# Gated linear attention beside a bilinear GLU: a new order for one unit's ScalarE and VectorE work

## The chip, the cores and the metric

The kernel runs on one core of a Trainium2 chip. The metric is the device time of one execution in microseconds (us), as the median of several runs. The engines are TensorE (PE in the profile; PEld is its loading of stationary operands), VectorE (DVE), ScalarE (ACT), GpSimd (POOL) and SyncE (SP). SP and POOL do almost nothing here but issue DMAs.

## The reference

The input `x` has 2048 rows of 512 numbers. Two branches read it, and a gate mixes them:

```
g = sigmoid((x * gate_w).sum(-1))
a = linear attention(x; wqkv, wo)        # 32 heads of 16; phi(t) = where(t > 0, t+1, exp(t)) + 1e-6
b = ((x @ w_gate) * (x @ w_up)) @ w_down # 512 -> 1792 -> 512
out = g * a + (1 - g) * b
```

All of it is float32. The linear attention needs `kv = phi(k)^T v` and `z = sum phi(k)` over all rows before any query can be finished; a query's result is `phi(q) kv / (phi(q) z)`.

## The kernel before, in words

**Precision.** A float32 operand is split into a high part, which TensorE's fast format `fp32r` can hold, and a low remainder. A split is one ACT instruction (`hi = src`) and one DVE instruction (`lo = src - hi`), and a product is three matmuls (`mm3`: high by high, low by high, high by low). So every operand that TensorE reads costs ACT and DVE something first.

**Phase 1** (to 93.85 us of the profiled span) goes over the 16 row tiles and builds `pk = phi(x wk)` and the four banks `gt = pk^T x`. It opens with `WARM` dummy matmuls on zeros (line 184) while the first weights arrive.

**Phase 2** is a list of 32 **units** (`order`, lines 124 to 130). The 2048 rows are taken as two pairs of chunks of 2 x 512 rows; for each pair there are 14 units of kind "f" (one 128-wide slice of `w_gate` and `w_up`) with two units of kind "q" (query weights) among them, at places 6 and 11. A unit (line 387) multiplies a 2 x 2 block matrix of weights with a 2 x 2 block matrix of `x` in the seven products of a Strassen-like scheme; the sums of blocks that it needs are formed by DMAs that add in flight. The names of the products and the PSUM banks they go to, in PE's order, are

| product | bank | what it needs first | what reads the bank |
|---|---|---|---|
| 2 | Y | | ACT `m2` (named `m` in the profile) |
| 3 | X | | DVE `R = X - m2` |
| 4 | Y | `m2` has read Y | ACT `cross[:, 0]` |
| 1 | R | `R` written | DVE `t = R + cross[:, 0]` |
| 5 | X | `R` has read X | DVE `S = t - X`, ACT `cross[:, 1]` |
| 6 | R | `t` has read R | DVE `cross[:, 1] = R * cross[:, 1]`, then `hh[:, 1]` on ACT, `hl[:, 1]` on DVE |
| 7 | S | `S` written | DVE `cross[:, 0] = S * cross[:, 0]`, then `hh[:, 0]` on ACT, `hl[:, 0]` on DVE |

`h` (`hh`, `hl`) is the split hidden state of the unit's 128 columns, chunk 0 and chunk 1. Between the products stand **down jobs** (`down`, line 372; matmuls named `pdn`): two units' `h` times their `w_down` rows for one tile of 128 rows, six matmuls into one bank, added to an accumulator in SBUF by one DVE instruction (`acc`). The eight jobs of two units take the four tiles of chunk 1 first. `shares` says how many jobs follow products 3, 4, 5 and the `S` step of each unit.

**Order.** Every engine executes its instructions in the order in which the program lists them (`pin`). Work that belongs to no product is put at named places of a unit with `later(n, place, fn)` and executed by `do(n, place)`; along a unit the places are e (after `R`), m and c (after product 4), d (before product 1), t (after `t`), s (before the last down jobs), r (between products 6 and 7) and end. The steps that the change touches are

- the weights of later units: `w_load` (SP loads `wr`, three of seven blocks), `w_add` (two ACT instructions make copies and a negative in `wr`, then a POOL DMA adds 640 KB onto it), `w_high` and `w_low` (split into `wch` on ACT and `wcl` on DVE, in three parts; part 2 holds the blocks of products 1, 6 and 7);
- `down_weights` (line 711): the split of the unit's `w_down` rows, `dh` on ACT and `dl` on DVE, at place c, from a single buffer `wdr`, whose next load is issued behind the split;
- the attention of a q unit n (line 567): the query features `phq`, their products with z summed through DRAM (`zq`, `terms`, `zt`), the reciprocal (`recip`, which also writes `den` to DRAM), four broadcast loads `rb` of it (`norm`), and four pairs `norm_high` / `norm_low` that scale and split the features to an `h` of their own;
- the `x` blocks of the second pair: sums formed early by `cb_load`, `x_add` and `cb_split` and parked in DRAM, either split already (`xpark`, two tensors) or not (`xsum`), and loaded during unit 15 (`reload`); those from `xsum` are split during unit 16.

Of the kernel before, what the change touches and what calls it, by code (L numbers as in the profile page):

```python
# [7 lines left out]
F32 = mybir.dt.float32  # L8
F32R = mybir.dt.float32r
AF = mybir.ActivationFunctionType  # L10
ALU = mybir.AluOpType
# [3 lines left out]
P = 128  # L15
S = 2048
D = 512
# [8 lines left out]
NPAIR = NC // 2  # L26
TPP = 2 * CH // P
EPS = 1e-6
WARM = 7
LEAD = 4  # L30
HB = 8
NH = 5
# [11 lines left out]
def gated_mix(ctx: ExitStack, tc, xt, xp, x, wqkv, wq, wq_add, wo, wgu, wgu_add, wdn, gate_w, out):  # L44
# [12 lines left out]
    def act(dst, src, func=AF.Copy, **kw):  # L57
        pin(nc.scalar.activation(dst, src, func, **kw))  # L58

    def tt(dst, a, b, op):  # L60
        pin(nc.vector.tensor_tensor(dst, a, b, op=op))  # L61
# [54 lines left out]
    nc.gpsimd.affine_select(out=m3, in_=m3, compare_op=ALU.is_ge, fill=0.0, base=DH - 1,  # L116
                            pattern=[[DH, P // DH], [0, DH]], channel_multiplier=-1)

    xpark = {i: [dram.tile([P, 2, CH], F32, name=f"xpark{i}{v}") for v in "hl"] for i in (2, 3)}
    xsum = {i: dram.tile([P, 2, CH], F32, name=f"xsum{i}") for i in (4, 1, 5, 6, 7)}  # L120
    wpark = [[dram.tile([P, D], F32, name=f"wpark{b}{v}") for v in "hl"] for b in range(KT)]


# [18 lines left out]
    def w_add(n):  # L142

        if n < len(order):
            _, kind, m = order[n]
            act(raws[n][:, 3:5], raws[n][:, 0:1].to_broadcast([P, 2, 2 * P]))
            act(raws[n][:, 5:7], raws[n][:, 0:2], scale=-1.0)
            dma_add(raws[n][:, 2:7], (wgu_add if kind == "f" else wq_add)[m])
# [3 lines left out]
    def w_high(n):  # L152
        if n < len(order):
            wcs[n] = [const.tile([P, 7, 2 * P], F32R, tag=f"wc{v}", name=f"wc{v}", bufs=2) for v in "hl"]
            for a, b in PARTS:
                act(wcs[n][0][:, a:b], raws[n][:, a:b])

    def w_low(n, part):
        if n < len(order):
            a, b = PARTS[part]  # L160
            tt(wcs[n][1][:, a:b], raws[n][:, a:b], wcs[n][0][:, a:b].bitcast(F32), ALU.subtract)
# [203 lines left out]
    def later(n, place, fn):  # L365
        at.setdefault((n, place), []).append(fn)

    def do(n, place):
        for fn in at.pop((n, place), []):
            fn()  # L370
# [16 lines left out]
    def unit(n, quad):  # L387

        wh, wl = wcs.pop(n)
        bank = {t: psum.tile([P, CH], F32, tag=t, name=f"b{t}") for t in "YXRS"}  # L390

        def reload(i):
            if n + 1 == units and i in xpark:
                for src, part in zip(xpark[i], xc[i]):
                    dma(part.bitcast(F32), src)
            elif n + 1 == units:
                hi, lo = xc[i]
                dma(lo.bitcast(F32), xsum[i])

                def split_there():  # L400
                    act(hi, lo.bitcast(F32))
                    tt(lo, lo.bitcast(F32), hi.bitcast(F32), ALU.subtract)

                later(units, {4: "e", 1: "m", 5: "c", 6: "t", 7: "s"}[i], split_there)

        def product(i, to, start=False):
            for k in range(2):
                ks = slice(k * P, (k + 1) * P)
                mm3(bank[to], (wh[:, SLOT[i], ks], wl[:, SLOT[i], ks]), [v[:, k] for v in xc[i]],
                    start and k == 0, k == 1, not start)  # L410
            reload(i)

        m2 = p2.tile([P, CH], F32, tag="t", name="m2")
        cross = p2.tile([P, 2, CH], F32, tag="cross", name="cross", bufs=2)
        product(2, "Y", True)
        act(m2, bank["Y"])
        product(3, "X", True)

        tt(bank["R"], bank["X"], m2, ALU.subtract)
        do(n, "e")  # L420
        many = share(n)
        down(many[0])
        product(4, "Y")
        act(cross[:, 0], bank["Y"])
        do(n, "m")
        do(n, "c")
        down(many[1])
        do(n, "d")
        w_add(n + 2)
        product(1, "R")  # L430
        t = p2.tile([P, CH], F32, tag="t", name="t")
        tt(t, bank["R"], cross[:, 0], ALU.add)
        if n:
            w_high(n + 1)
        do(n, "t")
        product(5, "X")
        tt(bank["S"], t, bank["X"], ALU.subtract)
        act(cross[:, 1], bank["X"])
        if n:
            w_low(n + 1, 0)  # L440
        down(many[2])
        if quad:
            quad(1, 0, cross[:, 0])
        if n:
            w_low(n + 1, 1)
        do(n, "s")
        down(many[3])
        w_low(n + 1, 2)
        if quad:
            quad(0, 1, cross[:, 1])  # L450
        product(6, "R")
        if quad:
            quad(1, 1, bank["R"])
        else:
            hh, hl = hidden()
            tt(cross[:, 1], bank["R"], cross[:, 1], ALU.mult)
            act(hh[:, 1], cross[:, 1])
        do(n, "r")
        product(7, "S")
        if quad:  # L460
            quad(0, 0, bank["S"])
        else:
            tt(cross[:, 0], bank["S"], cross[:, 0], ALU.mult)
            act(hh[:, 0], cross[:, 0])

            for c in 1, 0:
                def low(c=c):
                    tt(hl[:, c], cross[:, c], hh[:, c].bitcast(F32), ALU.subtract)

                if n + 1 == len(order):  # L470
                    later(n, f"low{c}", low)
                else:
                    low()
            return hh, hl

    def hidden():
# [8 lines left out]
    def wp_load():  # L485
        att["wv"] = [p2.tile([P, D], F32, tag="acc", name="wv", bufs=8) for _ in range(KT)]
        att["wo"] = [p2.tile([P, D], F32, tag="ph", name="wo_sb", bufs=4) for _ in range(KT)]
        for k in range(KT):
            dma(att["wv"][k], wqkv[k * P:(k + 1) * P, 2 * D:3 * D])
        for k in range(KT):  # L490
            dma(att["wo"][k], wo[k * P:(k + 1) * P, :])
# [76 lines left out]
    def attention(pair, j, n):  # L568
# [41 lines left out]
        def norm(i):  # L610
            r, c = parts[i]
            if r not in group:
                group[r] = hidden()
            rb = p2.tile([P, CH], F32, tag="z", name="rb", bufs=4)
            one = there[HB * i:HB * (i + 1)].rearrange("h c t -> h (c t)")
            dma(rb, one[:, None, :].to_broadcast([HB, DH, CH]))
            den[i] = rb
# [26 lines left out]
        for e, place in zip((1, 2, 3), ("s", "s", "end")):  # L644
            later(n + 2, place, lambda e=e: z_add(e))
        later(n + 2, "end", z_end)
        later(n + 3, "e", recip)
        for i in range(4):
            later(n + 3, "m", lambda i=i: norm(i))
        for i, places in enumerate((((n + 3, "r"), (n + 4, "e")), ((n + 4, "m"), (n + 4, "c")),  # L650
                                    ((n + 4, "d"), (n + 4, "t")), ((n + 4, "s"), (n + 4, "r")))):
            for fn, (m, place) in zip((norm_high, norm_low), places):
                later(m, place, lambda i=i, fn=fn: fn(i))
        later(*((n + 5, "e") if turns else (n + 3, "c")), weights)
# [10 lines left out]
    def cb_split(i, k):  # L665
        lo = cb.pop((i, k))
        if i in xsum:
            dma(xsum[i][:, k], lo)
            return
        hi = p2.tile([P, CH], F32R, tag="cb", name="cbh", bufs=3)  # L670
        act(hi, lo)
        tt(lo, lo, hi.bitcast(F32), ALU.subtract)
        dma(xpark[i][0][:, k], hi.bitcast(F32))
        dma(xpark[i][1][:, k], lo)
# [13 lines left out]
    for n, (i, k) in enumerate((i, k) for i in (2, 3, 4, 1, 6, 7) for k in range(2)):  # L688
        later(n, "s", lambda i=i, k=k: cb_load(i, k))
        later(n + 1, "c", lambda i=i, k=k: x_add(cb[i, k], 1, i, k))  # L690
        later(n + 2, "c", lambda i=i, k=k: cb_split(i, k))
    later(1, "r", lambda: dma(xsum[5], xp[1, SUMS[5][1]]))
    wdr = {}

    def d_load(n):
        if n < len(order) and order[n][1] == "q":
            n += 1
        if n < len(order):
            wdr[n] = p2.tile([P, D], F32, tag="wdr", name="wdr")
            dma(wdr[n], wdn[order[n][2]])  # L700

    d_load(0)
    wp_load()
    half = None
    for n, (pair, kind, m) in enumerate(order):
        entry = {}
        if n == 6:

            banks[0] = "att"

        def down_weights(n=n, entry=entry):
            entry["d"] = down_tiles()
            split(*entry["d"], wdr.pop(n))
            d_load(n + 1)

        if kind == "f":
            at.setdefault((n, "c"), []).insert(0, down_weights)
        hid = unit(n, attention(pair, m, n) if kind == "q" else None)
        w_load(n + 3)
        if kind == "f":  # L720
            if half is None:
                half = (hid, entry["d"])
            else:
                jobs += down_jobs(pair, (half, (hid, entry["d"])), ocol)
                half = None
        do(n, "end")
# [56 lines left out]
```

## Time and profile before

| what | value |
|---|---|
| median of 3 runs | 609.63 us (607.29 to 611.16) |
| the profiled execution | 611.52 us, of which the span from first to last instruction is 609.7 us |
| PE busy | 601.4 us, 99% of the span, 2657 matmuls |
| DVE busy | 443.2 us, 73% |
| ACT busy | 311.3 us, 51% |
| granted TensorE clock | 1.000 over the span |
| phase 2, first to last matmul | 93.85 to 606.2 us |

In a group's row the tile that is written stands left of the arrow, what is read right of it; "idle before" is the time for which the engine did nothing ahead of these instructions, with the instruction that ended it. In a timeline a row gives start, duration, engine, line and tiles, and in brackets the idle time ahead of it. Nearly all instructions go through helpers, so a line number tells little (L52 is every matmul, L58 every ACT copy, L61 every DVE subtraction or product) and the tile names have to be read.

### The profile page before, as it was taken

How to read it: one execution, taken by the hardware profiler on the slowest of the kernel's cores; microseconds unless marked ns; L12 is line 12 of the kernel's file. 1: busy time of each engine (PE TensorE's matmuls, PEld its weight loads, DVE VectorE, ACT ScalarE, POOL GpSimd, SP SyncE). 2: the span in 40 equal slices, each digit the busy share in tenths (PEclk: the TensorE clock that was granted, in tenths of full speed). 3: DMA queues.
4: the chain of work that ended last, by engine and by line, in shares of the span. 5: the costliest groups of instructions: out<-in, count | busy, mean ns of one | idle time of the engine just before them, and what ended most of it. 6: DMA issues, size and time to landing. Idle time of an engine off the chain costs nothing.

```text
span 609.7 us, 7505 instructions
## 1 busy us (share of the span) xinstructions
PE 601.4 (99%) x2657; PEld 494.7 (81%) x2657; DVE 443.2 (73%) x690; ACT 311.3 (51%) x533; POOL 46.4 (8%) x62
## 2 busy tenths in 40 slices
PE   9999999999999999899999999999999999999997
PEld 6888888888888888788887788888888887888886
DVE  6877896666776787767887876556677887668874
ACT  3855765476549542564444634664474455643310
POOL 0011100001111110200000012010000000000000
PEclk9999999999999999999999999999999999999999
DMA  9477956667777868857469725334476564552403
GB/s 300 164 186 134 285 147 145 184 173 205 209 186 175 234 130 237 200 131 198 103 148 307 231 95 156 88 90 87 85 188 163 117 166 103 136 138 57 140 0 139
DMA packets 48406, 96.97 MB, mean 159 GB/s; under 512 B 4448, under 2 KB 15456, under 8 KB 48352
## 3 DMA queue, kind: packets, MB, share of 16 engines
q1 hardware_dynamic: 40672, 67.65, 34.1%
q0 software_dynamic: 7408, 28.32, 26.1%
q10 hardware_dynamic: 288, 0.52, 0.3%
q8 instruction: 21, 0.34, 0.2%
q14 instruction: 17, 0.14, 0.1%
HBM read 81.53 MB, written 15.47 MB: 159 GB/s over the span
## 4 chain that ended last, share of the span: by engine, by line
PE 88%; DMA 4%; DVE 4%; ACT 1%; issue 1%
PE pdn L52 28%; PE bR L52 13%; PE bY L52 13%; PE bX L52 13%; PE pk L52 7%; PE gt L52 7%; PE bS L52 6%; DMA wdr<-in_wdn 4%; DVE acc L64 1%; DVE wcl L61 1%; DVE cross L61 1%; PE pkv L52 1%; DMA wraw<-in_wqkv 1%; DVE hl L61 1%; PE pw L52 0%
## 5 line engine op out<-in xcount | busy, mean ns | idle before, releaser
L52 PE MATMUL pdn<-dh,hl 128*128 128x512 f32 x290 | 112.5, 388 | 0.4 <-DVE hl L61 0.4
L52 PE MATMUL pdn<-dh,hh 128*128 128x512 f32 x290 | 112.5, 388 | 0.2 <-ACT hh L58 0.2
L52 PE MATMUL pdn<-dl,hh 128*128 128x512 f32 x290 | 112.4, 388 | 0.0
L58 ACT ACTIVATE hh<-cross 128x512 fp32r<-128x512 f32 x56 | 35.1, 633 | 98.1 <-DVE cross L61 98.1
L64 DVE SCALAR_TENSOR_TENSOR acc<-pdn,ocol,acc 128x512 f32<-128x512 f32 (+1 forms) x97 | 71.0, 738 | 13.2 <-PE pdn L52 11.6
L61 DVE TENSOR_TENSOR wcl<-wr,wch 128x512 fp32r<-128x512 f32 (+1 forms) x96 | 72.9, 773 | 1.8 <-ACT wch L58 1.8
L52 PEld LDWEIGHTS pdn<-dh,hl 128*128 128x128 f32 x290 | 54.4, 188 | 11.9 <-DVE hl L61 0.8
L52 PEld LDWEIGHTS pdn<-dh,hh 128*128 128x128 f32 x290 | 54.5, 188 | 11.8 <-ACT hh L58 0.6
L52 PEld LDWEIGHTS pdn<-dl,hh 128*128 128x128 f32 x290 | 54.5, 188 | 11.2
L58 ACT ACTIVATE wch<-wr 128x512 fp32r<-128x512 f32 (+1 forms) x96 | 60.0, 691 | 0.0
L58 ACT ACTIVATE cross<-bY 128x512 f32<-128x512 f32 x32 | 19.1, 598 | 68.0 <-PE bY L52 68.0
L61 DVE TENSOR_TENSOR dl<-wdr,dh 128x512 fp32r<-128x512 f32 x28 | 19.4, 692 | 44.2 <-ACT dh L58 44.2
L52 PE MATMUL bX<-xbh,wch 128*128 128x512 f32 x128 | 49.8, 389 | 0.0
L52 PE MATMUL bX<-xbh,wcl 128*128 128x512 f32 x128 | 49.8, 389 | 0.0
L52 PE MATMUL bX<-xbl,wch 128*128 128x512 f32 x128 | 49.8, 389 | 0.0
L85 POOL DMA_DIRECT2D wr<-in_wgu_add x28 | 24.3, 866 | 303.4 <-ACT wr L58 186.7
L61 DVE TENSOR_TENSOR hl<-cross,hh 128x512 fp32r<-128x512 f32 x56 | 37.9, 688 | 2.7
L58 ACT ACTIVATE wr<-wr 128x512 f32<-128x512 f32 x64 | 36.6, 622 | 4.4 <-DMA wr<-in_wgu 4.4
L61 DVE TENSOR_TENSOR bR<-bX,m 128x512 f32<-128x512 f32 x32 | 22.3, 697 | 15.2 <-PE bX L52 15.2
L61 DVE TENSOR_TENSOR bS<-t,bX 128x512 f32<-128x512 f32 x32 | 22.2, 695 | 15.1 <-PE bX L52 15.0
L58 ACT ACTIVATE cross<-bX 128x512 f32<-128x512 f32 x32 | 19.0, 593 | 25.1 <-DVE bS L61 25.0
L61 DVE TENSOR_TENSOR t<-bR,cross 128x512 f32<-128x512 f32 x32 | 22.0, 688 | 13.5 <-PE bR L52 13.5
(160 smaller groups left out, 1262.8 us busy)
## 6 DMA issues: line engine op xcount, KB each, us to landing
wr<-in_wgu_add POOLq DMA_DIRECT2D x28, 640.0 KB, 7.5
wr<-in_wgu SPq DMA_DIRECT2D x28, 384.0 KB, 5.7
wdr<-in_wdn SPq DMA_DIRECT2D x28, 256.0 KB, 4.9
xraw<-in_x SPq DMA_DIRECT2D x16, 256.0 KB, 4.8
terms<-zq SPq DMA_DIRECT2D x16, 256.0 KB, 2.3
zt<-terms SPq DMA_DIRECT2D x16, 256.0 KB, 8.2
rb<-den SPq DMA_DIRECT2D x16, 256.0 KB
xtraw<-in_xt SPq DMA_DIRECT2D x12, 256.0 KB, 4.1
```

What stands on the lines that cost most here:

```text
L52: tc.keep_in_program_order(nc.tensor.matmul(*args, **kw))
L58: pin(nc.scalar.activation(dst, src, func, **kw))
L61: pin(nc.vector.tensor_tensor(dst, a, b, op=op))
L64: pin(nc.vector.scalar_tensor_tensor(dst, a, scalar, b, op0=op0, op1=op1))
L85: tc.keep_in_program_order(nc.gpsimd.dma_start(dst, src, accum_op=ALU.add))
```

## The change

No matmul of the computation is added or removed. Within a unit the ACT and DVE work stands in another order:

- `hh[:, 0]` and `hl[:, 0]` of a unit move into the next unit: `hh[:, 0]` behind that unit's `m2`, `hl[:, 0]` behind its `R`. The last unit keeps the old order.
- `down_weights` moves from place c to place e, ahead of whatever else stands there; its load buffer `wdr` becomes two, and each load is issued two f units ahead.
- `w_high` moves ahead of `w_add` and of product 1; `w_low` of part 0 moves from behind product 5 to behind `t`.
- The attention's `recip` moves from place e of unit n + 3 to the end of n + 2, the `rb` loads from m to e, and each `norm_high` / `norm_low` one place or so earlier.
- The `x` block 4 of the second pair is split before it is parked and loaded as two tensors; its split in unit 16 goes. The splits of parked blocks (`cb_split`) move from c to e.
- There are 8 dummy matmuls at the start where there were 7.

```diff
-WARM = 7
+WARM = 8
...
-    xpark = {i: [dram.tile([P, 2, CH], F32, name=f"xpark{i}{v}") for v in "hl"] for i in (2, 3)}
-    xsum = {i: dram.tile([P, 2, CH], F32, name=f"xsum{i}") for i in (4, 1, 5, 6, 7)}
+    xpark = {i: [dram.tile([P, 2, CH], F32, name=f"xpark{i}{v}") for v in "hl"] for i in (2, 3, 4)}
+    xsum = {i: dram.tile([P, 2, CH], F32, name=f"xsum{i}") for i in (1, 5, 6, 7)}
...
-                later(units, {4: "e", 1: "m", 5: "c", 6: "t", 7: "s"}[i], split_there)
+                later(units, {1: "m", 5: "c", 6: "t", 7: "s"}[i], split_there)
...
         product(2, "Y", True)
         act(m2, bank["Y"])
+        do(n, "high")
         product(3, "X", True)
 
         tt(bank["R"], bank["X"], m2, ALU.subtract)
+        do(n, "low")
         do(n, "e")
...
         do(n, "d")
+        if n:
+            w_high(n + 1)
         w_add(n + 2)
         product(1, "R")
         t = p2.tile([P, CH], F32, tag="t", name="t")
         tt(t, bank["R"], cross[:, 0], ALU.add)
         if n:
-            w_high(n + 1)
+            w_low(n + 1, 0)
         do(n, "t")
         product(5, "X")
         tt(bank["S"], t, bank["X"], ALU.subtract)
         act(cross[:, 1], bank["X"])
-        if n:
-            w_low(n + 1, 0)
         down(many[2])
...
             tt(cross[:, 0], bank["S"], cross[:, 0], ALU.mult)
-            act(hh[:, 0], cross[:, 0])
-
-            for c in 1, 0:
-                def low(c=c):
-                    tt(hl[:, c], cross[:, c], hh[:, c].bitcast(F32), ALU.subtract)
-
-                if n + 1 == len(order):
-                    later(n, f"low{c}", low)
-                else:
-                    low()
+
+            def high(c):
+                act(hh[:, c], cross[:, c])
+
+            def low(c):
+                tt(hl[:, c], cross[:, c], hh[:, c].bitcast(F32), ALU.subtract)
+
+            if n + 1 < len(order):
+
+                low(1)
+                later(n + 1, "high", lambda: high(0))
+                later(n + 1, "low", lambda: low(0))
+            else:
+
+                high(0)
+                for c in 1, 0:
+                    later(n, f"low{c}", lambda c=c: low(c))
             return hh, hl
...
-        later(n + 3, "e", recip)
+        later(n + 2, "end", recip)
         for i in range(4):
-            later(n + 3, "m", lambda i=i: norm(i))
-        for i, places in enumerate((((n + 3, "r"), (n + 4, "e")), ((n + 4, "m"), (n + 4, "c")),
-                                    ((n + 4, "d"), (n + 4, "t")), ((n + 4, "s"), (n + 4, "r")))):
+            later(n + 3, "e", lambda i=i: norm(i))
+        for i, places in enumerate((((n + 3, "s"), (n + 3, "r")), ((n + 3, "end"), (n + 4, "e")),
+                                    ((n + 4, "c"), (n + 4, "d")), ((n + 4, "t"), (n + 4, "s")))):
...
-        later(n + 2, "c", lambda i=i, k=k: cb_split(i, k))
+        later(n + 2, "e", lambda i=i, k=k: cb_split(i, k))
...
-    def d_load(n):
-        if n < len(order) and order[n][1] == "q":
-            n += 1
-        if n < len(order):
-            wdr[n] = p2.tile([P, D], F32, tag="wdr", name="wdr")
+    ffn = [n for n, u in enumerate(order) if u[1] == "f"]
+
+    def d_load(i):
+        if i < len(ffn):
+            n = ffn[i]
+            wdr[n] = p2.tile([P, D], F32, tag="wdr", name="wdr", bufs=2)
             dma(wdr[n], wdn[order[n][2]])
 
     d_load(0)
     wp_load()
+    d_load(1)
...
-            d_load(n + 1)
+            d_load(ffn.index(n) + 2)
 
         if kind == "f":
-            at.setdefault((n, "c"), []).insert(0, down_weights)
+            at.setdefault((n, "e"), []).insert(0, down_weights)
```

## The prediction

> **What bounds the kernel now.** I read the busy shares first, then PE's list of waits, then the timelines around each wait.
>
> ```profile
> PE 601.4 (99%) x2657; PEld 494.7 (81%) x2657; DVE 443.2 (73%) x690; ACT 311.3 (51%) x533; POOL 46.4 (8%) x62
> ```
> ```profile
> PE bY L52 <- ACT m L58: 2.1, 2, 1.8
> ...
> PE bY L52 <- DVE xc4l L61: 0.6, 1, 0.6
> PE pdn L52 <- DVE hl L61: 0.4, 1, 0.4
> ```
>
> PE is busy 99% of the span, and the chain of waits shows six matmuls every 1.36 us (0.227 each) from 7.33 us on. The change leaves every real matmul, so only time in which PE does not keep this pace can be won. Start to start, all distances over 0.227 add up to 8.3 us: 3.1 before 7.33 us (slow clock, first weights), 0.5 in six small hitches, and 4.7 in three places of phase 2. Behind PE's last matmul lie 3.5 us of accumulation and output, unchanged. No order of ACT and DVE can win more than 4.7 + 0.5 in phase 2.
>
> ```profile
> 252.72 0.39 PE L52 MATMUL pdn<-dh,hl 128*128 128x512 f32 x1
> 254.87 0.50 PE L52 MATMUL bY<-xc4h,wch 128*128 128x512 f32 x1 [1.77 <-ACT m L58]
> 255.21 0.39 PE L52 MATMUL bY<-xc4l,wch 128*128 128x512 f32 x1
> ...
> 334.93 0.50 PE L52 MATMUL pdn<-dh,hh 128*128 128x512 f32 x1 [0.20 <-ACT hh L58]
> ...
> 336.06 0.50 PE L52 MATMUL pdn<-dh,hl 128*128 128x512 f32 x1 [0.40 <-DVE hl L61]
> ...
> 338.82 0.50 PE L52 MATMUL bY<-xc4l,wch 128*128 128x512 f32 x1 [0.65 <-DVE xc4l L61]
> ...
> 507.94 0.50 PE L52 MATMUL bY<-xc4h,wch 128*128 128x512 f32 x1 [0.31 <-ACT m L58]
> ```
>
> Each stall costs more than its bracket, since the pipeline refills. At 254.87: 255.21 - 252.72 is 2.49 for two steps of 0.227, so 2.03 lost. The other places, counted so: 1.15 (334.34 to 336.40), 0.92 (338.82) and 0.59 (507.94). Together 4.7. They are the starts of units 11, 16 and 27: each follows a unit that holds the attention's norm work, where DVE is at its limit.
>
> ```profile
> 241.31 0.69 DVE L61 TENSOR_TENSOR dl<-wdr,dh 128x512 fp32r<-128x512 f32 x1 [2.18 <-ACT dh L58]
> ...
> 252.99 0.68 DVE L61 TENSOR_TENSOR cross<-bS,cross 128x512 f32<-128x512 f32 x1
> 253.59 1.47 DVE L61 TENSOR_TENSOR hl<-cross,hh 128x512 fp32r<-128x512 f32 x2
> 254.97 0.69 DVE L61 TENSOR_TENSOR bR<-bX,m 128x512 f32<-128x512 f32 x1
> ```
> ```profile
> 253.70 0.63 ACT L58 ACTIVATE hh<-cross 128x512 fp32r<-128x512 f32 x1 [0.57 <-DVE cross L61]
> 254.24 0.58 ACT L58 ACTIVATE m<-bY 128x512 f32<-128x512 f32 x1
> ```
>
> Product 4 of unit 11 waits for `m2`. Its input (product 2) was done at 250.38, but on ACT it stands behind `hh[:, 0]`, which waits for `cross[:, 0]` on a late DVE. DVE is late because it stood idle 2.18 us in unit 10 for `dh`, and 1.26 more for `wch`. In units 15 and 26 the `dl` idle is 3.08 and 1.72.
>
> **Part by part.** *`h` of chunk 0 in the next unit.* Nothing is added. ACT reads Y before it touches `hh[:, 0]`, DVE writes `R` one instruction (0.61 from start to start) earlier. At 254.24 this alone gives `m2` 0.54. First reader of the late half: a chunk-0 job. Four chunk-1 jobs always come first; in unit 16, where ten jobs follow at once, the first chunk-0 job is the seventh, 5.4 us after `hl[:, 0]`. Hidden. New wait: `hh[:, 0]` may hold `dh` and `cross[:, 0]` behind it on ACT, where `t` waits for the latter; that needs a DVE that is 4 us late. Cost 0.
>
> *The `w_down` split at e, two buffers.* The group `dl<-wdr,dh` has 44.2 us of idle DVE time in 28 instructions, 1.58 each. Behind `hl[:, 0]`, with `dh` 0.6 us behind `m2`, it waits for nothing. Recount of unit 15 in the new order: 15 DVE instructions at 0.61, five `acc` at 0.66 and one `wcl` of 0.87 are 13.3 us against 16.32 of PE. Walked through, its last `hl` ends 17.7 us after its start (332.5); the job that stalled at 334.34 needs it there. In units 10 and 26 the same walk brings `hh[:, 1]` and then `m2` 2 to 3 us earlier, more than 1.8 and 0.6. So the stalls of units 11 and 27 and the two at 334 to 336 go: -3.8.
>
> *Block 4 parked in split form.* The stall on `xc4l` goes: -0.9. Price: four more DVE/ACT instructions of 0.62 to 0.69 in units 6 and 7 and one more 512-KB load in unit 15. The operand is due at 336.6, its loads can issue near 320.5, and the same kind (`xc1l`) landed after 7.2. Hidden.
>
> *`w_high` ahead of `w_add`.* Before, the 640-KB add of a unit went out before the previous weights were split; now a loop closes: add lands, three `wch` (2.07), two `wr` (1.25), POOL issue (0.87), landing (6 to 9.1). That is 10.2 to 13.3 us per unit; units last 14.96 or more, only units 6, 7, 22 and 23 last 12.24. There it slips up to 1.1 us twice, on ACT and then `wcl` and `S`, while product 7 leaves `S` 2.7 us. Cost 0 (to 0.5).
>
> *The norm steps earlier.* This adds a dangerous wait: `norm_high(1)` now stands at the end of units 9, 14, 25 and 30, so on ACT `hh<-rb` precedes the next `m2`, and `rb` is a DMA.
>
> ```profile
> 225.79 2.70 SPq L82 DMA_DIRECT2D rb<-den  x4
> 228.59 0.63 SPq L82 DMA_DIRECT2D wdr<-in_wdn  x1
> ```
> ```profile
> 233.99 0.69 DVE L64 SCALAR_TENSOR_TENSOR rb<-phq,rb 128x512 f32<-128x512 f32 x1 [1.86 <-DMA rb<-den]
> ```
>
> The first `rb` takes 8.2 us. Unit 10 starts at 232.44; its product 4 comes at 236.52; `rb` to `hh` to `m2` takes 1.9; so the second `rb` must land by 234.6. Before, the SP instruction that waited for it issued at 236.28: at that time it would cost 1.7. Now `recip` runs some 2 us earlier (without `hl[:, 0]` and `R` before it, one `wcl` moved), so `rb` issues near 223.8, while POOL's add, behind three `wch`, starts about 1.7 us later. That matters: from 228 to 231 SP's queue moved 41 packets beside 96 of the add; with no add (562 to 565) it moved 207. Against it, `wdr` and a parking store now stand ahead of `rb`. I put the landing between 232 and 235.5, the cost in unit 10 at 0.5 (0 to 1.7). In units 14 and 25 no parking store is left (1.4 us less ahead), in unit 30 there is no add: 0 (to 1.7 each). The Trainium skill (DMA: Bandwidth & Descriptors, Queues, rings and completion order) says each DMA engine consumes one queue's descriptors in ring order; this speaks against the change, and the row above agrees: the `wdr` issued at 310.75 behind four `rb` took 12.6 us against a median of 4.9. By that rule alone, with two transfers of 1.4 us ahead, the second `rb` would land near 237 and the sum would be 1.9 us worse.
>
> *The eighth dummy.* Dummies start every 0.427 us; the seventh starts at 3.79, the eighth would run 4.22 to 4.65, and the first real matmul started at 4.66 behind an idle 0.23. Cost 0 (from 1.3 gained, below, to 0.4 lost).
>
> **Sum.** -3.8 - 0.9 + 0.5 = -4.2. Against the profiled execution: 611.52 (span 609.7 and 1.8 around it) to 607.3. That execution is 1.9 above the median; the stalls come from fixed orders, so I take the same 4.2 off the median: **605.4**.
>
> **Rivals.** *The stall moves to `rb`.* If `rb` lands as late as before, 1.7 in the three rounds with an add is 5.1, and 4.7 is given back: 610.0. For: the row at 233.99 and the same waits in units 14 (1.29) and 25 (1.84). Against: the issue 2 us earlier.
>
> *Slower by the same wait.* The point where it decides: the second `rb` landing 3.6 us past its due time in three rounds costs 10.8 - 4.7 = 6.1, so 615.8. That is 238.2, 14 us behind its issue; the longest load behind `rb` took 12.6. For: everything on ACT, `m2` too, would stand behind a DMA in a jammed queue.
>
> *Faster by the clock.* Matmuls run 0.427 apart until 7.33. If the idle 0.23 us before 4.66 held the clock back, the eighth dummy could win the time from 4.66 to 7.33 less six normal steps: 1.3 us, so 604.1. Against: the pace rose by 7.33 although that gap lay before it. The Trainium skill (TensorE: Matmul & The Clock Gate, Part 1) says that the clock is released by a busy window of about 3.4 us that runs freely, not reset by the kernel; by that rule filling one gap moves the rise only by chance.
>
> **Chances.** A measurement of this kernel tells about 1% (6.1 us) from no change. Forecast 0.70; stall moves 0.12; slower 0.10; clock 0.08. Runs of one kernel spread by 4 us, so 0.06 of the forecast and half of the clock case fall below 603.5: faster 0.10, same 0.80, slower 0.10. The range 603.2 to 610.0 holds the forecast with its spread, most of the clock case and half of the moved stall.
>
> **What would show it.** Right: no idle time of PE at the starts of units 11, 16 and 27; `dl` with under 10 us of idle DVE time; no `m` among PE's releasers but for at most 1 us near 236.5. Wrong: `m` waiting for `hh<-rb` in units 10, 15 or 26; ACT's `wch` waiting for the add by over 3 us; a `bR` or `bS` among PE's waits.

## The result, and the profile after

The changed kernel takes 605.29 us as the median of seven runs (605.03 to 607.12), the kernel before 608.78, also of seven; the ratio is 0.9945 with a 95% interval of 0.9925 to 0.9964. In a later set of six runs it took 605.41 (605.25 to 606.57) against 610.49 of seventeen, ratio 0.9926 (0.9906 to 0.9946). So it is faster by 3.5 us in the first set and by 5.1 in the second (3.4 and 4.5 by the ratios), under the 1% that the prediction named as its bound. The forecast was 605.4 in a range of 603.2 to 610.0, and "within 1%" had the chance 0.80.

Here are the busy shares of the changed kernel and PE's list of waits (releaser, us in all, times, the longest). The one wait that is left in the list is at the start of the kernel; none is in phase 2:

```profile
PE 600.1 (99%) x2658; PEld 495.3 (82%) x2658; DVE 440.5 (73%) x691; ACT 309.2 (51%) x534; POOL 46.4 (8%) x62
```
```profile
PE warm L52 <- DVE xc1h L109: 1.3, 1, 1.3
```

The timeline of PE at the four places that stalled before: product 4 of unit 11, the first down job of unit 16, the product with `xc4l` in unit 16, product 4 of unit 27.

```profile
252.84 0.39 PE L52 MATMUL pdn<-dh,hl 128*128 128x512 f32 x1
253.07 0.39 PE L52 MATMUL bY<-xc4h,wch 128*128 128x512 f32 x1
253.29 0.39 PE L52 MATMUL bY<-xc4l,wch 128*128 128x512 f32 x1
...
331.72 0.39 PE L52 MATMUL bX<-xbh,wcl 128*128 128x512 f32 x1
331.95 0.39 PE L52 MATMUL pdn<-dh,hh 128*128 128x512 f32 x1
332.18 0.39 PE L52 MATMUL pdn<-dl,hh 128*128 128x512 f32 x1
...
334.67 0.39 PE L52 MATMUL bY<-xc4h,wch 128*128 128x512 f32 x1
334.89 0.39 PE L52 MATMUL bY<-xc4l,wch 128*128 128x512 f32 x1
...
503.08 0.39 PE L52 MATMUL pdn<-dh,hl 128*128 128x512 f32 x1
503.31 0.39 PE L52 MATMUL bY<-xc4h,wch 128*128 128x512 f32 x1
```

From start to start there are 0.22 or 0.23 us in all four places; the bracket with the idle time is gone from each row. The view of the tile `wdr` has no idle time of DVE any more, where it had 44.2 us before. The slowest of its loads took 12.6 us before; now the line is

```profile
DMA to landing us min/median/max: 2.7/3.0/3.2
```

The bookkeeping of the two profiled executions (611.52 and 606.59 us, so -4.93): the start of phase 2 moved from 93.85 to 94.04 (+0.19), phase 2 from its first to its last matmul shrank from 512.37 to 507.41 (-4.96), and the tail from 3.51 to 3.33 (-0.18). (The tail goes with block 4: 3.32 to 3.34 in the six executions that park it in split form, 3.50 to 3.52 in the eight others. Why is open.) In phase 2 the distances over 0.24 us between matmuls, less 0.227 each, added up to 5.16 and add up to 0.39. I call this sum the **loss** below. It is the figure to compare in single executions, since the start of phase 2 moves by itself: in the fourteen profiled executions of this study it lay anywhere from 92.8 to 95.0.

### The profile page after: what moved, and what is told of

Same layout as the page of the kernel before. It is cut to its first block, busy times and chain, and to the rows that moved or that the text cites. A ratio compares the mean times of both kernels' runs of the same rounds, so it can differ in the third digit from the quotient of the medians.

```text
span 604.8 us, 7551 instructions
## 1 busy us (share of the span) xinstructions
PE 600.1 (99%) x2658; PEld 495.3 (82%) x2658; DVE 440.5 (73%) x691; ACT 309.2 (51%) x534; POOL 46.4 (8%) x62
## 4 chain that ended last, share of the span: by engine, by line
PE 99%; DVE 0%; issue 0%
PE pdn L52 32%; PE bY L52 14%; PE bX L52 14%; PE bR L52 14%; PE pk L52 7%; PE bS L52 7%; PE gt L52 7%; PE warm L52 1%; PE pkv L52 1%; PE pw L52 0%; PE pz L52 0%; DVE acc L64 0%; DVE xc1h L109 0%
## 5 line engine op out<-in xcount | busy, mean ns | idle before, releaser
L64 DVE SCALAR_TENSOR_TENSOR acc<-pdn,gcol,acc 128x512 f32<-128x512 f32 x32 | 23.7, 749 | 17.3 <-PE pdn L52 17.1
L58 ACT ACTIVATE m<-bY 128x512 f32<-128x512 f32 x32 | 19.1, 596 | 23.5 <-PE bY L52 23.3
```

The source lines that it names most:

```text
L64: pin(nc.vector.scalar_tensor_tensor(dst, a, scalar, b, op0=op0, op1=op1))
```

## The experiments

The four kernels from "h alone" to "h and w_down" were run once each beside one run of the kernel before (608.62 us), the four from "old norm places" to "`rb` later" likewise on another chip (608.80), and the last four rows on a third. All numbers but the medians are of one profiled execution.

| kernel | time | start of phase 2 | phase 2 | loss |
|---|---|---|---|---|
| before | 611.52 | 93.85 | 512.37 | 5.16 |
| after | 606.59 | 94.04 | 507.41 | 0.39 |
| h alone | 605.73 | 92.85 | 507.58 | 0.51 |
| w_down at e, two buffers, alone | 606.88 | 92.81 | 508.86 | 1.75 |
| w_down at e, one buffer, alone | 605.48 | 92.87 | 507.38 | 0.35 |
| h and w_down (two buffers) | 606.57 | 93.64 | 507.71 | 0.70 |
| after, old norm places | 605.98 | 93.01 | 507.92 | 0.87 |
| after, old block 4 | 606.20 | 93.20 | 507.77 | 0.70 |
| after, old weights' order | 613.34 | 92.79 | 515.41 | 8.31 |
| after, `rb` later | 621.58 | 93.34 | 523.21 | 16.14 |
| before again | 610.72 | 93.72 | 511.78 | 4.55 |
| after again | 605.33 (median 605.41) | 93.03 | 507.18 | 0.18 |
| one buffer again | 605.51 (median 607.34) | 92.86 | 507.44 | 0.36 |
| after, `m2` first | 607.20 (median 605.65) | 94.97 | 507.19 | 0.18 |

### h of chunk 0 in the next unit, alone

```diff
         act(m2, bank["Y"])
+        do(n, "high")
...
         tt(bank["R"], bank["X"], m2, ALU.subtract)
+        do(n, "low")
...
-            act(hh[:, 0], cross[:, 0])
+                low(1)
+                later(n + 1, "high", lambda: high(0))
+                later(n + 1, "low", lambda: low(0))
```

> The kernel before with one part of the change: chunk 0's h in the next unit, nothing else. Before, PE lost 2.0 us at the start of unit 11, 1.15 in the first down jobs of unit 16, 0.9 on xc4l there and 0.6 at the start of unit 27, 4.7 together. My theory (VectorE runs late in the norm units because it sits idle for dh; the order of h adds little): m2 comes 0.54 us earlier and no more, so 1.5 stay at unit 11, nothing at unit 27, the first jobs of unit 16 keep their 1.15 (chunk 1's hl keeps its place) and xc4l its 0.9: about 3.6 of 4.7 us stay. The rival (m2 queued behind hh of chunk 0 is the cause): unit 11 and unit 27 lose nothing any more, 2 us stay.

Measured in one execution: nothing was left of the stalls but 0.24 us at `xc4l`. My theory, by which this order gives `m2` only 0.54 us, fell. The timeline of ACT and DVE at the end of its unit 10 and the start of unit 11; of PE's rows only product 4's first is shown:

```profile
249.75 0.68 DVE L61 TENSOR_TENSOR cross<-bR,cross 128x512 f32<-128x512 f32 x1
250.35 0.68 DVE L61 TENSOR_TENSOR hl<-rb,hh 128x512 fp32r<-128x512 f32 x1
250.46 0.63 ACT L58 ACTIVATE hh<-cross 128x512 fp32r<-128x512 f32 x1 [2.15 <-DVE cross L61]
250.95 0.68 DVE L61 TENSOR_TENSOR cross<-bS,cross 128x512 f32<-128x512 f32 x1
251.00 0.58 ACT L58 ACTIVATE m<-bY 128x512 f32<-128x512 f32 x1
251.55 0.68 DVE L61 TENSOR_TENSOR hl<-cross,hh 128x512 fp32r<-128x512 f32 x1
251.66 0.63 ACT L58 ACTIVATE hh<-cross 128x512 fp32r<-128x512 f32 x1
...
251.75 0.40 PE L52 MATMUL bY<-xc4h,wch 128*128 128x512 f32 x1
```

`m2` now stands right behind `hh[:, 1]`, 0.54 after its start. In the kernel before, `hh[:, 1]` began at 252.50 and `m2` at 254.24, 1.74 later: between them lay not only the other `hh` but also ACT's wait for `cross[:, 0]`. So the order gives 1.74 - 0.54 = 1.20, not 0.54. That is still less than the idle time of 1.77 at 254.87. The rest came from the landing of `wdr`: set against PE's matmuls, `dl` of unit 10 started 0.85 us earlier than in the kernel before, and 1.20 + 0.85 is the 2.05 by which `m2` came earlier. In unit 15 `dl` waited 1.64 where it had waited 3.08. Unit 16's first down jobs do not depend on the order of `hh[:, 0]` at all: they wait for `hh[:, 1]` and `hl[:, 1]`, which stand ahead of chunk 0's in both orders. So the 1.15 that this execution won there is not the order's. Whether landings differ so by themselves, the kernel before had to tell.

### The kernel before, again

No edit.

> The kernel before once more, for the spread of its own stalls. In the first profile DVE stood 2.18, 3.08 and 1.72 us for dl in units 10, 15 and 26, and phase 2 lost 5.2 us to distances over 0.227. The alone-h kernel, with the same order of DMAs, had 1.76 and 1.64 us in units 10 and 15 and lost 0.5. If the landing of w_down behind the four rb loads is fixed by the order of issue: all three waits within 0.3 us of the first profile, and 4.9 to 5.4 us lost. If the landing varies from execution to execution: at least one of the three waits is off by over 0.5 us, the stalls at the starts of units 11, 16 and 27 change with it, one for one, and part of what the alone-h kernel won was such a variation.

In its timeline, `dl` of unit 10 and product 4 of unit 11:

```profile
240.30 0.69 DVE L61 TENSOR_TENSOR dl<-wdr,dh 128x512 fp32r<-128x512 f32 x1 [1.24 <-ACT dh L58]
...
253.83 0.50 PE L52 MATMUL bY<-xc4h,wch 128*128 128x512 f32 x1 [0.79 <-ACT m L58]
```

`dl` waited 1.24 where it had waited 2.18 (0.94 less) and PE stood 0.79 where it had stood 1.77 (0.98 less). In unit 15 it was 2.65 against 3.08, in unit 26 1.80 against 1.72, and there PE's idle time went from 0.31 to 0.39. So the second expectation holds: the landing behind the four `rb` varied by up to a microsecond between two executions of one program, and the stall followed one for one. Beside that, unit 26 had a loss of 0.55 at its own product 4 (490.21), where DVE had waited 2.32 us for the first `rb`. So of what the kernel with h alone won, 1.20 at the start of unit 11 belongs to its order, and so does unit 27, where `dl` waited 2.03 and nothing was lost; the rest belongs mostly to that execution's landings. It was run once, and what it loses with the landings of before was not seen.

### The w_down split at e, with two buffers and with one

```diff
-            at.setdefault((n, "c"), []).insert(0, down_weights)
+            at.setdefault((n, "e"), []).insert(0, down_weights)
```

```diff
+            wdr[n] = p2.tile([P, D], F32, tag="wdr", name="wdr", bufs=2)
...
-            d_load(n + 1)
+            d_load(ffn.index(n) + 2)
```

The kernel with one buffer has the first of these edits alone, the other both.

> The kernel before with the w_down split at place e and two load buffers, nothing else. My theory: dl's idle VectorE time falls from 44 us to under 10, VectorE runs 2 to 3 us earlier in units 10, 15 and 26, and the stalls of units 11 and 27 and of the first jobs of unit 16 are gone although m2 still stands behind hh of chunk 0; 0.5 to 0.9 us stay on xc4l. So at most 1 of 4.7 us stays. The rival (the order of m2 and hh): at least 2 us stay at the starts of units 11 and 27.

> As the kernel with the w_down split at place e, but with the single load buffer of before. If the place of the split is what counts, the same as with two buffers: at most 1 us of the 4.7 stays, since the load then issues ahead of the four rb loads in the norm units. If the second buffer is what counts (the wdr load that landed 12 us after its issue), dh waits for its load in units 10, 15 and 26 by 1 to 2 us and at least 2 us of stalls stay.

In both, `dl` waits for nothing (44.2 us before), so it is the place of the split that counts; no run shows a gain from the second buffer. The stalls in unit 16 are gone, the one on `xc4l` too, though I had expected that one to stay. With two buffers product 4 of units 11 and 27 still lost 0.67 and 0.87, which I had not expected. Its timeline of ACT and PE:

```profile
242.75 1.15 ACT L58 ACTIVATE wr<-wr 128x512 f32<-128x512 f32 x2 [2.05 <-DMA wr<-in_wgu]
...
251.57 0.58 ACT L58 ACTIVATE m<-bY 128x512 f32<-128x512 f32 x1
...
252.20 0.50 PE L52 MATMUL bY<-xc4h,wch 128*128 128x512 f32 x1 [0.40 <-ACT m L58]
```

Where the wait for `w_down` is gone, the next DMA in line becomes the wait: ACT stands 2.05 us for the load of the next weights (`wr`), and `wch`, DVE's `wcl` and the unit's `cross` stand behind it. Before, the late DVE hid all but 0.89 of this. With one buffer it was 1.52, and `m2` ended at 251.67, when product 4 was due at 251.70: 0.1 us lost, and nothing to spare. The two kernels differ here by 0.5 us in the landing of one load, which is less than the 0.94 that another load varied by itself. In the changed kernel ACT's largest idle time at a `wr` or `wch` in or behind a norm unit is 0.26 us, since the weights' steps stand elsewhere.

### One buffer again, and the changed kernel again

> The kernel before with only the place of the w_down split changed, single buffer. In its first profile phase 2 lost 0.35 us. If this one move is the whole gain: ratio 0.992 to 0.997, within 0.002 of the changed kernel on the same chip, phase 2 loses under 0.7. If the first profile was a lucky one (the kernel with two buffers, otherwise the same, lost 1.75): 1.0 to 2.0 us lost, ratio 0.002 to 0.003 above that of the changed kernel.

> The changed kernel once more, beside the two that follow. If its stalls are fixed by the order: phase 2 loses 0.2 to 0.6 us (0.39 in the first profile), with one hitch of 0.2 near 236.6; ratio 0.9925 to 0.9964. If landings vary by 1 us and more, one of units 10, 15, 26, 31 shows product 4 late on m2 by up to 1 us, since bR waits 1.18 us for m2 there and nothing is left.

The profiles repeat themselves (loss 0.36 and 0.18). The times do not agree with them: the one-line kernel had a median of 607.34 in twelve runs, from 605.35 to 610.67, ratio 0.9951 (0.9931 to 0.997); the changed kernel 605.25 to 606.57. The ratios' intervals overlap, but in 64 of the 72 pairs of one run of each the changed kernel is the faster. So the one line is the whole gain in its best executions and 3.2 of 5.1 us in the median (610.49 to 607.34, against 605.41), and the other parts together buy evenness; which of them does was not tested. Both profiled executions of the one-line kernel lie at the low end of its times; where its slower ones lose was not seen. That it is the `m2` of units 11 and 27, which has nothing to spare there, is only argued.

### Both together, without the rest

The two edits above (with two buffers) in the kernel before.

> The kernel before with both parts, chunk 0's h in the next unit and the w_down split at e with two buffers; weights, norm steps, block 4 and dummies as before. My theory: units 11 and 27 and the first jobs of unit 16 lose nothing, the stall on xc4l stays with 0.5 to 0.9 us, so phase 2 is 3.8 to 4.2 us shorter than before. If the gain came from the other parts (norm steps, weights), 2 us or more stay.

Loss 0.70, of which 0.52 at `xc4l` in unit 16. Beside h, the 0.67 and 0.87 are gone, but with `w_down` alone nothing was lost at `xc4l`. With h, `hl[:, 0]` stands on DVE ahead of the split of block 4, beside `dl`. At the starts of units 11 and 27 the two parts work on the same stalls, so what each takes away alone does not add up.

### Block 4 unsplit

```diff
-    xpark = {i: [dram.tile([P, 2, CH], F32, name=f"xpark{i}{v}") for v in "hl"] for i in (2, 3, 4)}
-    xsum = {i: dram.tile([P, 2, CH], F32, name=f"xsum{i}") for i in (1, 5, 6, 7)}
+    xpark = {i: [dram.tile([P, 2, CH], F32, name=f"xpark{i}{v}") for v in "hl"] for i in (2, 3)}
+    xsum = {i: dram.tile([P, 2, CH], F32, name=f"xsum{i}") for i in (4, 1, 5, 6, 7)}
...
-                later(units, {1: "m", 5: "c", 6: "t", 7: "s"}[i], split_there)
+                later(units, {4: "e", 1: "m", 5: "c", 6: "t", 7: "s"}[i], split_there)
```

> The changed kernel with block 4 parked whole and split in unit 16 again. My theory: VectorE is no longer late there, but the split of 1.05 us on ScalarE and 1.22 on VectorE stands behind m2, hh and dh, and R, hl and dl, so its low part ends about 6.0 us after the unit's start where PE wants it after 5.67: 0.4 to 0.6 us lost on xc4l, nothing else. If the 0.9 us of before came from the late VectorE alone: 0. If it is the split's own length: 0.9.

Loss 0.70, and 0.51 of it at `xc4l` (334.26), as expected. That step is real in the changed order, though smaller than the 0.92 that stood there before. It is needed only beside h: with `w_down` alone, block 4 was split in unit 16 as before, and nothing was lost there.

### The old places of the norm steps

```diff
-        later(n + 2, "end", recip)
+        later(n + 3, "e", recip)
...
-            later(n + 3, "e", lambda i=i: norm(i))
+            later(n + 3, "m", lambda i=i: norm(i))
```

The places of the four norm pairs are those of before as well; everything else is as after.

> The changed kernel with reciprocal, rb loads and norm steps at their old places. My theory (the norm steps give nothing; their new place costs 0.2 us at 236.6 because hh<-rb stands ahead of m2): no stall at the starts of units 11, 16 and 27, and the hitch of 0.2 us in unit 10 is no larger; VectorE waits 1 to 2 us for rb again in units 9, 14 and 25, hidden. Phase 2 within 0.3 us of the changed kernel. The rival (earlier norm steps are needed to take VectorE's load off the end of the norm units): 1 us or more of stalls at units 11, 16 or 27.

Loss 0.87, of which 0.69 at product 4 of unit 10 (236.05), where the first `rb` step on DVE had waited 3.06 us for its DMA. The early places were worth about 0.5 us in this execution, in one round of four. I had expected nothing (within 0.3 us), and the rival 1 us or more; it is neither.

### The old order of the weights

```diff
         do(n, "d")
-        if n:
-            w_high(n + 1)
         w_add(n + 2)
         product(1, "R")
...
         tt(t, bank["R"], cross[:, 0], ALU.add)
         if n:
-            w_low(n + 1, 0)
+            w_high(n + 1)
```

and `w_low` of part 0 behind product 5 again.

> The changed kernel with the weights' steps in the old order: the add is issued before the next weights are split, and the low part 0 comes behind product 5. My theory: this part of the change neither gives nor costs anything, phase 2 within 0.3 us of the changed kernel, no stall over 0.3 us anywhere. The rival (the loop of add and split costs, or the earlier split is what relieves VectorE): a difference of over 1 us one way or the other.

I had expected nothing of this order, and the one execution without it lost 8 us more. The timeline around unit 10:

```profile
223.67 2.54 SPq L82 DMA_DIRECT2D rb<-den  x4
...
223.88 0.87 POOL L85 DMA_DIRECT2D wr<-in_wq_add  x1 [11.48 <-ACT wr L58]
...
233.39 0.69 DVE L64 SCALAR_TENSOR_TENSOR rb<-phq,rb 128x512 f32<-128x512 f32 x1 [4.70 <-DMA rb<-den]
...
237.92 0.68 DVE L64 SCALAR_TENSOR_TENSOR rb<-phq,rb 128x512 f32<-128x512 f32 x1
...
238.64 0.63 ACT L58 ACTIVATE hh<-rb 128x512 fp32r<-128x512 f32 x1 [1.77 <-DVE rb L64]
239.17 0.58 ACT L58 ACTIVATE m<-bY 128x512 f32<-128x512 f32 x1
...
239.81 0.65 PE L52 MATMUL bY<-xc4h,wch 128*128 128x512 f32 x1 [4.35 <-ACT m L58]
```

The same rows in the changed kernel:

```profile
224.89 2.54 SPq L82 DMA_DIRECT2D rb<-den  x4
...
226.89 0.87 POOL L85 DMA_DIRECT2D wr<-in_wq_add  x1 [11.41 <-ACT wr L58]
...
230.19 0.69 DVE L64 SCALAR_TENSOR_TENSOR rb<-phq,rb 128x512 f32<-128x512 f32 x1 [0.28 <-DMA rb<-den]
...
234.72 0.68 DVE L64 SCALAR_TENSOR_TENSOR rb<-phq,rb 128x512 f32<-128x512 f32 x1
...
235.44 0.63 ACT L58 ACTIVATE hh<-rb 128x512 fp32r<-128x512 f32 x1 [1.77 <-DVE rb L64]
...
235.98 0.58 ACT L58 ACTIVATE m<-bY 128x512 f32<-128x512 f32 x1
...
236.59 0.70 DVE L61 TENSOR_TENSOR bR<-bX,m 128x512 f32<-128x512 f32 x1 [1.18 <-ACT m L58]
236.61 0.50 PE L52 MATMUL bY<-xc4h,wch 128*128 128x512 f32 x1
```

With the old order POOL's add goes out 0.21 us behind the first `rb`, with the new one 2.00 behind it, since `wch` precedes it; the first `rb` then takes 9.7 us to DVE instead of 5.3. What lies between is in the packets: from 226 to 230 us the add's queue moved 110 of them in the kernel with the old order and SP's queue, with `rb`, only 48; in the changed kernel SP's queue moved 464 in the same stretch and the add's queue none, since its packets came only about when the first `rb` was in. From the first `rb` step on DVE is never idle here: the second `rb` step stands 4.53 behind the first in both kernels, and `m2` 1.25 behind that, so `m2` starts 5.78 or 5.79 after the first `rb` step, as long as the second `rb` is in by then. The rounds with an add in five kernels (the add's start against the first `rb` issue; from that issue to the first `rb` step on DVE, by which the load was in; DVE's wait for it):

| kernel, round | add after `rb` issue | `rb` to DVE | DVE waited |
|---|---|---|---|
| before 1, 2, 3 | -0.23, -0.24, -0.21 | 8.20, 7.62, 8.19 | 1.86, 1.29, 1.84 |
| old norm places 1, 2, 3 | -0.32, +0.37, +0.53 | 8.00, 5.54, 5.70 | 3.06, 0, 0 |
| old weights' order 1, 2, 3 | +0.21, +0.46, +0.47 | 9.72, 5.17, 5.19 | 4.70, 0, 0 |
| later `rb` (next section) 1, 2, 3 | -0.01, +2.20, +0.31 | 9.26, 5.14, 9.82 | 6.24, 0, 6.48 |
| after 1, 2, 3 | +2.00, +2.21, +2.23 | 5.30, 5.16, 5.18 | 0.28, 0, 0 |

Where the add went out from 0.3 us ahead of `rb` to 0.3 us behind it, `rb` took 2.3 to 4.6 us longer to DVE than in the changed kernel; with the add 2 us behind, DVE hardly waited. In the kernels with `w_down` at e the add went out 1.3 to 1.6 us ahead, and there it was 6.0 to 6.9 us to DVE. Between 0.3 and 2 us behind it is open: at +0.37 to +0.53 the first `rb` came in time, but at one +0.47 DVE waited 1.67 for the second, and unit 26 lost 1.6 us.

### The `rb` loads four DMAs later

```diff
-            later(n + 3, "e", lambda i=i: norm(i))
+            later(n + 3, "d", lambda i=i: norm(i))
```

> The changed kernel with the four rb loads behind the four loads of the attention's output weights (place d for e), so that they land some 4 times 1.4 us later in units 9, 25 and 30; in unit 14 nothing stands between, so it is the control. My theory of the dangerous wait: the first rb step moves from 230.2 to about 235.8, the second follows it 4.5 us later on VectorE, hh<-rb stands ahead of m2 on ScalarE, and m2 is already at its due time in the changed kernel; so PE loses 4 to 8 us at product 4 of units 10, 26 and 31 each, waiting for m, and nothing in unit 15: 12 us or more slower in all. The rival (m2 has cover of its own): under 1 us in each.

PE's list of waits:

```profile
PE bY L52 <- ACT m L58: 12.0, 2, 6.1
```

For units 10 and 26 the add is at -0.01 and +0.31 of the `rb` issue, `rb` takes 9.3 and 9.8 us, and product 4 stands 5.9 and 6.1. In unit 15, where the add follows after 2.20, and in unit 31, which has none though the same four loads stand ahead of `rb`, nothing happens. The wait that the prediction called dangerous exists, and with place d the one execution took 12.8 us longer than the kernel before beside it (608.80). It struck only where the add went out beside it; that it would strike in three units was wrong.

### `m2` ahead of the second norm step

```diff
-WARM = 8
+WARM = 7
...
-        for i, places in enumerate((((n + 3, "s"), (n + 3, "r")), ((n + 3, "end"), (n + 4, "e")),
+        for i, places in enumerate((((n + 3, "s"), (n + 3, "r")), ((n + 4, "e"), (n + 4, "c")),
```

> The changed kernel with norm_high(1) at place e of unit n + 4 (behind m2 on ACT) in place of the end of n + 3, norm_low(1) at c, and 7 dummies. If hh<-rb ahead of m2 is the only thing that holds m2 in the norm units: bR waits under 0.7 us for m2 there (1.18 before), the hitch of 0.2 at 236.6 goes, phase 2 loses 0.1 to 0.3; with some 0.2 us from the dummy, 0.3 to 0.4 us less than the changed kernel, ratio 0.9935 to 0.9945, which is not to be told from it. If the later norm step makes the rest of the norm work late instead: the hitch moves to product 7 or to unit 11's first down jobs, 0.5 to 1 us, and the ratio is 0.0005 to 0.0015 above that of the changed kernel.

From the list of DVE's waits, the changed kernel and then this one:

```profile
DVE bR L61 <- PE bX L52: 30.6, 22, 1.9
...
DVE bR L61 <- ACT m L58: 4.7, 4, 1.2
```
```profile
DVE bR L61 <- PE bX L52: 34.3, 26, 1.5
```

The wait of `bR` for `m2` in the four norm units is gone: `bR` waits for PE there, as everywhere else. But PE had hardly been waiting for it: 605.65 us, ratio 0.9927 (0.9904 to 0.9949), not to be told from the changed kernel's 605.41 in the same set. No version here beats it.

## Why the prediction was right, and where its steps were not

**What bounds the kernel, and how much there is to win: right.** The stalls added up to 5.2 in phase 2; the change took 4.8 of them. That the median came out within 0.2 us of the forecast is in part luck: the forecast took 4.2 off a median of 609.63, and with seven runs the kernel before stands at 608.78, so 3.5 us were won in that set and 5.1 in the other. The reason given for taking 4.2 off, that the stalls come from fixed orders, does not hold: the loss of the kernel before was 5.16 in one execution and 4.55 in the next. The marks it gave for "right" are all there: no idle time of PE at the starts of units 11, 16 and 27, no idle `dl`, and at `m` one hitch of 0.2 us at 236.6 in one execution and none in the other.

**`h` in the next unit, "alone 0.54": mis-sized.** It is 1.20. I counted `hh[:, 0]` ahead of `m2`, but not the 0.57 for which that instruction itself waited and the spacing behind it; the row of `hh` at 253.70 showed it in its bracket. It cost nothing, as said.

**The `w_down` split, -3.8: the sum right, the attribution not.** Removing `dl`'s wait suffices in the best executions: the loss was 0.35 and 0.36 with one buffer, and the stall on `xc4l`, which I had put down to block 4, went with it. At units 11 and 27 h works on the same stalls. What the step left out is what is late next: with the split moved and h not, ACT's wait for the next weights' load in unit 10 was 1.2 to 2.1 us where it had been 0.9, and 1.5 us of PE's time came back in one execution. I had taken DVE's idle time as fixed; it varied by about 1 us with the landing.

**Block 4, -0.9: mis-sized.** In the changed order it is 0.5. With `w_down` alone it would have been nothing: there no time is lost at `xc4l` although block 4 is split in unit 16.

**`w_high` ahead of `w_add`, "cost 0 (to 0.5)": right as a cost, wrong as a whole.** The loop of 10.2 to 13.3 us that I added up slipped nowhere: `wch` waits for no add in the changed kernel. (ACT does stand 1.58 and 0.84 us near 212 and 462, but for the load, as it stood 1.76 near 211 before.) But I had put the gain of this order into a half-sentence of another step ("starts about 1.7 us later. That matters") and no price on it. The 1.7 is right: the add stands 1.75 to 1.79 us later against `rb` than in the old order. In the one execution without it, 8 us hang on it, 6.2 of them in one unit, once the norm steps stand early.

**The norm steps, 0.5 (0 to 1.7): right in size (0 and 0.2), wrong in the point.** I set the due time for the second `rb` at 234.6. With the new places the second step on DVE stands 4.53 behind the first, so what decides is the first `rb`. It was due at about 230.1 (product 4 at 236.52, less 5.79 to the start of `m2` and 0.6 for it); it came at 230.19 in one execution, with the hitch of 0.2, and 0.36 earlier against PE in the other, with none. The slack is that small. What holds it is that with the add 2 us behind, the first `rb` step started 4.9 to 5.3 us after the issue in every round. The issue came at 224.89, not at 223.8. By the rule of the Trainium skill on ring order (DMA: Bandwidth & Descriptors, Queues, rings and completion order), read alone, the second `rb` should have landed near 237, behind `wdr` and a parking store. It was in by 234.72, when DVE took it without waiting. The same section says that each DMA engine takes turns between the queues that have work; the table above agrees with that as far as it goes, since the late rounds go with the add on POOL's queue and not with what stood ahead of `rb` on SP's. The 12.6 us of the `wdr` issued at 310.75, which I took as a sign of the ring order, stood behind such an add as well (issued at 307.97): behind four `rb` with no add, the `wdr` issued at 563.88 took 6.9.

**The eighth dummy, 0, and the rival of the clock: no gain seen.** With eight dummies the first real matmul began at 4.83 to 4.98, with seven at 4.66 to 5.02. The last distance of 0.427 us ended anywhere from 4.8 to 7.2 us with eight (six executions) and from 4.8 to 9.0 with seven (eight executions). Phase 2 began at 92.8 to 94.0 with eight and at 92.8 to 95.0 with seven, so 1.3 us would hardly show. That the pace rises at another time in each execution agrees with the Trainium skill (TensorE: Matmul & The Clock Gate, Part 1: The HAM clock gate), by which the clock's window runs freely.

**The rivals of `rb`** did not come about in the changed kernel. They are real in its neighbours, each run once: the old weights' order (613.34, a loss of 8.31 against 5.16 and 4.55) and the later `rb` (621.58, 16.14) lose more than the kernel before by that very wait.

## What to carry to other kernels

When an engine's idle time behind a DMA is removed, list the DMAs that the same engine reads next and ask when each lands now; parts that relieve one late engine work on the same stalls, so test each alone, and more than once, before adding their gains. What a reordering is worth can lie in the collision that it avoids: a small load that the critical chain waits for should be issued well ahead of a large add on another queue (2 us here), not beside it. Compare executions in number before trusting one profile, since a kernel with little slack and one with enough can show the same best trace.

## What the hardware showed that was not expected

After a long idle time PE comes back at half pace. In the kernel with the old weights' order, the busy time of each engine and the granted clock in three stretches (length, then PE, PEld, DVE, ACT and POOL with their counts, the clock, the DMA share, GB/s): idle, just behind the stall, and after it.

```profile
237.50:239.80 2.30, 0.00 (x0) 0.00 (x0) 1.12 (x3) 1.16 (x3) 0.00 (x0) 1.00 0.70 268
239.80:243.70 3.90, 3.90 (x10) 3.08 (x11) 3.74 (x6) 1.71 (x4) 0.87 (x1) 0.56 0.33 116
243.70:246.00 2.30, 2.30 (x12) 1.89 (x11) 1.53 (x3) 2.30 (x5) 0.46 (x1) 1.00 1.02 253
```

The clock is 0.56 on average for 3.9 us behind the stall, in which matmuls start 0.427 apart, so the 4.35 us of idle time cost 6.2 in all. The two stalls of 5.9 and 6.1 us in the kernel with the later `rb` did the same and cost 7.5 and 8.4, while no stall up to 1.77 us did it in any kernel. In the first of the two, the clock fell while PE was still idle:

```profile
236.00:237.90 1.90, 0.00 (x0) 0.00 (x0) 1.90 (x4) 0.63 (x1) 0.00 (x0) 1.00 0.53 204
238.00:241.80 3.80, 0.00 (x0) 0.00 (x0) 2.64 (x5) 1.75 (x4) 0.86 (x1) 0.50 0.45 167
```

PE's last matmul ended there at 235.95, so the clock fell after 2.0 us of idle time (in the second stall it fell after 3.6 us, in the kernel with the old weights' order only as the stall ended). The Trainium skill (TensorE: Matmul & The Clock Gate, Part 1: The HAM clock gate) puts the limit at about one window of 3.4 us of idle time. The lengths of the stalls fit that, with none between 1.8 and 4.3; the fall after 2.0 us does not. What a stall between 1.8 and 4.3 us costs, no run shows. So the price of a wait ahead of TensorE is not linear: the long ones cost 1.6 to 2.3 us more than their idle time, the one of 1.77 only 0.3.

The second surprise is how much one execution differs from the next at fixed order: 0.94 us in the landing of one load, one for one in PE's stall, and in the start of phase 2 2.2 us with seven dummies and 1.3 with eight.
